# A block-attention and Fourier-mixing kernel: its instruction order replaced as a whole, some e^s - 1 ops and one clear given to GpSimd

## The chip, the cores and the metric

The kernel runs on one core of a Trainium2 chip. The metric is device time in microseconds of one launch. A core has five engines that run side by side and meet through semaphores: TensorE (PE, with weight loads shown apart as PEld), VectorE (DVE), ScalarE (ACT), GpSimd (POOL) and SyncE (SP), which here only issues DMAs. GpSimd issues DMAs too, and each engine takes its instructions in program order.

## The reference, cut to what matters

There are four batches, eight heads, 768 positions and 64 features per head. The first half is attention within blocks of 96 positions, whose keys and values are first mixed across the eight blocks by a Sinkhorn-normalised 8 x 8 matrix P.

```python
for _ in range(5):
    P = exp(P - max(P)); P = P / sum(P, -1); P = P / sum(P, -2)
k_sorted = einsum('bhij,bhjcd->bhicd', P, k_b)
v_sorted = einsum('bhij,bhjcd->bhicd', P, v_b)
attn = softmax(0.125 * q_b @ k_sorted.T)      # inside each block
x = attn @ v_sorted                           # to [4, 768, 512]
```

The second half mixes x by a two-dimensional Fourier transform, normalises each position and adds a feed-forward.

```python
u = x + real(fft(fft(x, axis=1), axis=2))
un = (u - mean(u)) / sqrt(var(u) + 1e-06)
out = u + maximum(un @ w_ch1, 0) @ w_ch2      # 512 -> 2048 -> 512
```

## The kernel before, in words

The work is written as small steps, each a Python generator named `t_` and a letter; each `yield` cuts it into calls. A string ORDER of 1314 tokens says which step is called next; a token such as `x010` makes the next call of step x with the arguments 0, 1, 0. Trailing capital letters choose an engine: A is ScalarE, D is VectorE, P is GpSimd. At the end (the loop over `runs`) every instruction is tied to the one before it on its engine, so ORDER fixes the order of work on TensorE, VectorE, ScalarE, SyncE and GpSimd alike. A second string, SLOTS, gives each tile that is taken from a shared pool its buffer (the eight PSUM banks b0 to b7 among them).

The steps, with the lines that the profile names:

- Sinkhorn (L316 to L324): a chain that alternates between VectorE and ScalarE on a 32 x 64 matrix pw, which SyncE loads first. Two copies of it, pdup (L378, L381), feed J (L389) and D (L448) on TensorE, from which B, T, H and b make the block-diagonal mixing matrices.
- I (L277): two filler matmuls on the identity, which wait for one of Sinkhorn's ten normalisations: `I4` for number 4, and so on. Their result is not used.
- M, Z, s (L425, L432, L463): the mean of v over a block and v minus that mean. The tile vst holds v in two halves of 48 positions, loaded by L229; V loads the second pair of batches.
- v, w (L476, L486, copies at L286 and L288): mixed values into vsf. k (L511) and its copies: mixed keys. q (L306, or L297 and a DMA transpose): transposed queries.
- x (L529, L534): scores on TensorE and their exponential ex on ScalarE, two heads at a time. e (L548): ex - 1, written to the buffer eb in 16 bits; the part that the 1 stands for comes back through an extra row. o (L561, L570, L575): the product with the values, a reciprocal of the sum and the scaled result in r.
- a, A, R, r, f, c, d, p, g: the Fourier parts. f folds r into sums and differences, c and d are the transforms on TensorE (L719, L755, L758), with a reversal of y on VectorE (L739); d leaves u (L769), p copies a part of PSUM (bs, L776) and adds and subtracts it (L782, L784) on the engine of its letter, and g takes the statistics (L791, L795).
- l, n: the norm, four small ops on GpSimd (L799 to L808) and un on ScalarE or VectorE (L816, L819), then a transpose into ut.
- h, y: the feed-forward. h (L843) is four matmuls of 384 columns for one of sixteen slices of the hidden width, evicted through a ReLU by ScalarE (L852) or VectorE (L850); y (L863) is four matmuls of 512 columns, the last of four adds u (L868) and stores. The last tile of all is done as four pieces of 128 columns.
- C loads tables and weights: `C0` the table dtab, its copy on GpSimd (L357), then the four parts of w1 and of w2; `C1` tab, `C2` cs, `C3` lt and rrow. L loads q and k of batches 2 and 3. GpSimd issues the loads of v, q, k, w1 and w2; SyncE the rest.

eb has four buffers, one for each head modulo four. Their zeros around the blocks are set once: three by VectorE (L246), the first instructions that it has, and one by GpSimd (L258). Behind L258, GpSimd sets some constants and issues the loads of q and k of batch 1 (kq, L203).

Digits in a token are batch, head pair (or head, or half) and index: `h00i` is batch 0, half 0, slice 8. Batches overlap: attention of one stands beside the feed-forward of the one before.

Of the kernel before, what the change touches and what calls it, by code (L numbers as in the profile page):

```python
# [18 lines left out]
H = 8  # L19
# [87 lines left out]
def kernel(  # L107
# [18 lines left out]
        "00011101 00010234 50671030 12436570 13541602 05240031 63725241 "  # L126
        "61012052 63475001 25314102 06103012 04513222 10030415 11274602 "
        "53130145 36510210 03210302 01560420 33200075 60111221 22340330 "
        "01276225 10173200 00200653 04210013 13610004 56102525 11621110 "
        "65112701 35471623 05243052 00016450 16110470 21112364 21160323 "  # L130
        "61172420 61372041 64161010 20345245 17630010 04176325 11271652 "
        "37261401 05032102 33560171 00310010 00620057 32036401 11017624 "
        "23213156 23520605 43101204 47051106 01110521 03411070 16502411 "
        "02713260 50732415 00274113 52224760 11003511 22104731 00001210 "
        "17315000 14236220 31041230 03107652 01103651 01547162 30400762 "
        "37631401 07521240 11101501 01641320 27614031 54302100 11023201 "
        "50262732 36000054 07001001 51143120 04353542 00117102 16572110 "
        "40111035 60270456 07453147 352041 "
# [27 lines left out]
    def start(ins):  # L166
        return tc.keep_in_program_order(ins)
# [77 lines left out]
    for n in range(NE - 1):  # L245
        nc.vector.memset(ebuf[n][0:96, :], 0.0)  # L246
# [11 lines left out]
    start(nc.gpsimd.memset(ebuf[NE - 1][0:96, :], 0.0))  # L258
# [281 lines left out]
    def t_e(b, hp, g):  # L540
        for h2 in range(2):
            if h2:
                yield
            e = ebuf[(2 * hp + h2) % NE]
            ed = bass.AP(
                tensor=e.tensor, offset=e[:, S * g:S * g + 1].offset,
                ap=[e[0:96, :].ap[0], [224, 4], [1, BLK]])
            nc.vector.tensor_scalar(ed, exs[b, hp, g, h2], -1.0, None,  # L548
                                    op0=ALU.add)
# [330 lines left out]
    def t_i():  # L880
# [4 lines left out]
        "C0 I4 I5 M00 M01 M02 M03 J M04 M05 C0 B0 C1 B1 B2 D q00A Z0 "  # L885
        "Z0 s02 k00AA H k01AD Z0 s03 q00 k00 k00 k00 x001 k01 b0 s01 "
        "x000 x001 s04 b0 x000 x000 a0 a0 x001 s05 s00 q01D k01 q02D "
        "k01 k02AA q01 e001 k02 k02 v61A v61 v40A e001 v70A v40 v41D "
        "v50D a0 b1 k02 v41 q02 v30A v30 x010 V x010 x010 V T1 v70 "
        "v20A e010 v20 v50 e000 e000 e010 A0 R0 x011 x021 R0 R0 R0 "  # L890
        "q03D q03 R0 R0 x011 x011 x021 v60D v10A v60 v00A k10AA v10 "
        "e011 e011 x021 k03AA R0 v00 x020 x020 k03 k03 k03 o00 o01 "
        "k10 k10 k10 x020 e021 x030 o00 e020 x030 x030 e021 o02 o01 "
        "o00 o01 o03 o02 o03 x031 q11A r1 C2 C3 r0 r1 e030 o03 e020 "
        "o04 k11AA x031 e031 x031 o05 e030 R0 o04 e031 o04 q11 k11 R0 "
        "o02 o05 k11 q10A q13A q13 v51A o07 o07 o05 q10 v51 M10 o06 "
        "v31A k11 x111 x101 x101 x101 v31 M11 o07 o06 f00 o06 f00 "
        "v21A v01A f01 f01 k13AA e101 x110 f02 k13 f02 M12 M13 e101 "
        "f03 f03 M14 v21 x100 x111 x110 x111 e110 c00 L20 f04 x100 "
        "x110 c00 b1 L30 M15 C0 L20 q20 C0 f05 f05 Z1 v01 C0 e111 "  # L900
        "e110 c01 c01 c02 c00 e111 c01 c02 c03 c04 e100 r0 r0 v71A "
        "k12AA c03 q20 c04 d02 v71 v11A x100 d02 p02P d00 p02 d01 k12 "
        "q12A k12 e100 d00 c03 p00P p01P q12 v11 k13 d02 c04 d00 d01 "
        "Z1 c02 d04 p00 k12 k13 d01 p02 p01 p01 p04P Z1 I1 p00 d05 T2 "
        "g02 g01 p05P x121 x121 x131 x131 a1 o13 o10 a1 x121 g00 g01 "
        "x131 C0 g02 g00 l00 l00 l00 l00 e121 o12 I2 x130 e131 o11 "
        "d04 o12 d05 x130 x130 d05 d04 k20AA n001AA o11 q21 I3 e130 "
        "o11 d03 n001 n002AA n001 L21 n000DD o16 n002 p04 o12 n000 "
        "n000 L21 C0 p04 o16 p05 C0 n002 x120 x120 d03 k20 e130 p03P "
        "o13 s15 e120 o13 h00iA h00fD h00f h00i x120 o10 s10 o10 "  # L910
        "h00jD h00j e121 d03 h00cA h00pA h00hA h00h h00p q21 o16 "
        "h00dA e120 k21AA k21 s13 k21 k20 k20 h00c h00kD e131 s12 s14 "
        "x200 k21 h00oA h00nA s11 o14 x200 h00d x200 h00gA o17 h00aA "
        "h00k h00a h00lA wpA h00g p05 C0 o17 o17 o15 h00mA h00bA g05 "
        "o15 o14 o14 wkA h00l h00b wk h00n h00eA h00e o15 f10 h00o wp "
        "y0010 y0020 e200 g04 x201 x201 L30 x211 x211 p03 p03 g03 f11 "
        "f11 g04 f10 f12 h00m C0 g05 g03 l01 f12 e200 f13 y0021 y0022 "
        "l01 l01 x201 weD wbA wb wgD c10 we y0023 l01 q22 f13 n011DA "
        "e201 c10 f14 woA c11 c11 wo y0000 wjD e211 wj x211 y0001 "
        "n011 n011 c12 wg f15 whA wdA y0011 y0002 c13 c12 wh y0023 "  # L920
        "y0023 r1 n012DD f15 n012 y0012 wlA n012 c13 y0013 wcA q22 "
        "wnD waA wa n010DD n010 wl y0003 n010 wd c14 c14 h01aA wn "
        "y0003 wfD q23 q23 T3 y0013 c10 d11 h01oA h01o wiA h01dD h01d "
        "h01lA h01l y0003 y0013 d10 h01pA wc h01a wi h01p wf h01jD "
        "wmD h01gA wm e201 x210 d10 d10 c11 h01g x210 x210 p10P h01j "
        "d12 h01mA k22AD k22 k22 k22 e210 e210 k23DD q31 k23 k23 "
        "h01cA c13 d11 p12P h01c h01hA h01h p11P k23 h01fA h01f e211 "
        "h01iA d12 h01bD d12 p11 h01m h01i h01kA x230 x231 d11 h01b "
        "p12 p12 p11 g11 g12 g11 g12 x220 h01eA x230 h01e x220 x230 "
        "y0110 o22 x231 e231 o20 h01nD h01n o20 h01k o21 p10 p10 o23 "  # L930
        "o23 o20 L31 x220 L31 g10 g10 o23 y0111 y0112 y0120 a1 l10 "
        "l10 l10 l10 o22 o22 y0121 k31AA c14 n101A k31 q31 e230 e220 "
        "A1 c12 x231 o21 o21 k31 x221 n101 R1 e231 R1 n100A n100 "
        "y0100 y0101 q30 R1 R1 R1 n102A n102 x221 y0113 y0113 d13 "
        "y0102 y0122 R1 R1 e230 y0113 x221 e221 k31 d14 R1 R1 r2 r2 "
        "h10iA h10nA h10i d14 q30 k30DD e221 k30 k30 k30 y0123 r2 "
        "e220 y0123 p14P o27 h10eD h10n h10e h10kD o27 d14 y0123 "
        "y0103 d15 o27 h10aA h10a h10dA h10gA h10g h10bA y0103 h10k "
        "p13D p15P h10cA h10c h10hA h10mA h10m h10d q32 d13 d13 y0103 "
        "h10lA h10h h10jD p13 p14 p14 g14 d15 d15 g14 p15 p15 h10fA "  # L940
        "h10f h10oA o26 g15 p13 g13 g13 g15 l11 l11 l11 h10j o26 "
        "h10pD o26 h10b y1010 l11 o24 o24 y1000 h10l o25 n110D o25 "
        "h10o h10p y1011 x311 x311 x311 x301 f21 o25 f21 y1001 n112A "
        "x301 y1020 y1021 o24 f20 f20 n110 r3 e301 n111D y1002 y1012 "
        "f22 f22 f23 f23 c20 c20 y1013 y1022 q32 x300 x301 x300 x310 "
        "y1023 c21 c21 n112 f24 f25 c23 n111 e311 q33 y1013 y1023 c23 "
        "h11cD c22 f25 y1003 y1003 y1023 y1003 c22 c24 x300 h11c c24 "
        "k32DD k33DA k33 k33 e311 x310 k32 k32 d21 k33 p21P k32 d21 "
        "d21 e300 h11fD h11f h11oA e310 d22 d20 p20P h11lA p22P d22 "
        "d22 c24 h11mA c20 r3 h11kA q33 y1013 d20 h11l h11o p22 p22 "  # L950
        "h11m x310 h11hD h11jA h11j g22 o32 x331 e300 x331 h11bA p21 "
        "h11h x331 h11k g22 o32 h11eA h11iA e310 p20 c23 e301 p21 g21 "
        "h11b o32 h11pD h11aD h11a h11e h11i d20 p20 g20 g20 e331 "
        "x330 g21 l20 l20 l20 l20 h11p x321 h11gA h11g h11dA o31 x321 "
        "o30 o31 o31 e321 x321 h11nA h11d n202A y1110 x330 c22 o33 "
        "h11n y1111 y1112 n202 o33 e330 e331 c21 n201A o33 n201 n200D "
        "n200 r3 y1100 y1101 e321 x320 x320 e320 y1113 y1113 o30 "
        "y1120 x320 x330 e330 y1102 y1103 y1121 y1122 y1123 y1103 "
        "h20nA h20aA h20dD h20a d24 p24P y1123 y1123 d24 d24 d23 h20n "
        "h20lD h20l h20pD h20kD p23P h20k o30 h20jA h20j y1103 d25 "  # L960
        "d25 p24 p24 p25P g24 h20fD h20f h20p h20cA h20iD y1113 o34 "
        "h20c h20bA h20b h20eD d23 d23 d25 h20d p23 e320 h20mD o35 "
# [79 lines left out]
```

## Time and profile before

| | before |
|---|---|
| median of 4 runs | 272.01 us (271.62 to 272.39) |
| the profiled execution | 272.08 us, its span 270.3 us |
| busy: PE, DVE, ACT, POOL | 253.4, 197.1, 126.0, 74.7 us |
| share of the span | 94%, 73%, 47%, 28% |
| instructions of PE, DVE, ACT, POOL | 2440, 489, 287, 118 |
| mean granted TensorE clock | 0.987 |
| first h00 matmul | 62.36 us |
| chain that ended last | PE 85%, DVE 9%, ACT 3% |

The costliest groups are the feed-forward's matmuls: L843, 512 of 326 ns in the mean and 89.8 us busy, and L863, 432 of 355 ns and 88.6 us. Matmuls are pipelined, so that a duration is longer than the step from one to the next; four of L843 follow each other in 0.65 us. The e ops, L548, are 64 of 374 ns on VectorE, 22.9 us. The page's rows give line, engine, operation and shapes, then the busy time and the mean of one, then the idle time of the engine ahead of them and what ended it.

### The profile page before, as it was taken

Reading aid. Unit: us, or ns where it says so; the run is one execution under the profiler, and the core shown is the slowest. Engines: PE = TensorE matmul, PEld = TensorE weight load, DVE = VectorE, ACT = ScalarE, POOL = GpSimd, SP = SyncE. Lnnn points to the kernel's source line nnn. Section 1 sums busy time; section 2 is a strip of 40 time slices with the busy share of each in tenths; the row PEclk is TensorE's granted clock in tenths of the full one; section 3 lists DMA queues with packets and bytes.
Section 4 is the critical chain, followed back from the end, with each engine's and each line's share of the span. In section 5 each row is a group of like instructions: output and inputs, shape, how many; then the busy total and the mean of one; then the engine's idle time right before and its main releaser. Section 6 shows DMA issues by size and latency. Waiting matters only on the chain.

```text
span 270.3 us, 6119 instructions
## 1 busy us (share of the span) xinstructions
PE 253.4 (94%) x2440; PEld 157.2 (58%) x2440; DVE 197.1 (73%) x489; ACT 126.0 (47%) x287; POOL 74.7 (28%) x118
## 2 busy tenths in 40 slices
PE   0789889798999999999999999999999999999995
PEld 0279776565656766655655665466466545545554
DVE  6797999989999578868688696458965825912523
ACT  2258898985676476352633565133314312431100
POOL 8912400578721006502220053024200521410000
PEclk9977999999999999999999999999999999999999
DMA  6999999959980231843022610230023023020006
GB/s 120 204 250 205 217 242 242 183 89 174 207 129 14 62 110 29 119 102 83 37 49 45 116 37 10 57 116 4 19 42 116 0 44 133 0 42 19 0 12 223
DMA packets 33138, 26.38 MB, mean 98 GB/s; under 512 B 17395, under 2 KB 28787, under 8 KB 33108
## 3 DMA queue, kind: packets, MB, share of 16 engines
q0 software_dynamic: 11712, 13.63, 30.1%
q1 hardware_dynamic: 21398, 12.36, 17.5%
q8 instruction: 19, 0.31, 0.5%
q14 instruction: 9, 0.07, 0.1%
HBM read 29.00 MB, written 6.29 MB: 131 GB/s over the span
## 4 chain that ended last, share of the span: by engine, by line
PE 85%; DVE 9%; ACT 3%; issue 1%; POOL 1%; DVEq 0%
PE pf L863 31%; PE pf L843 29%; PE pf L719 3%; PE pf L561 3%; PE pf L529 2%; PE pf L425 2%; PE pf L755 2%; PE pf L511 2%; PE pf L758 2%; DVE eb L548 2%; PE pf L277 1%; PE pf L486 1%; PE pf L476 1%; PE pf L306 1%; PE pf L615 1%
## 5 line engine op out<-in xcount | busy, mean ns | idle before, releaser
L843 PE MATMUL pf<-ut,w1sb 128*128 128x384 f16 x512 | 89.8, 326 | 0.2
L863 PE MATMUL pf<-w2sb,hr 128*128 128x512 f16 (+1 forms) x432 | 88.6, 355 | 0.0
L843 PEld LDWEIGHTS <-w1sb 128*128 128x128 f16 x512 | 48.8, 98 | 31.2
L852 ACT ACTIVATE hr<-pf 128x384 f16<-128x384 f32 x78 | 35.7, 493 | 60.3 <-PE pf L843 60.1
L863 PEld LDWEIGHTS <-hr 128*128 128x128 f16 x432 | 38.5, 98 | 37.7
L782 POOL TENSOR_TENSOR u<-u,bs 128x255 f32<-128x255 f32 x21 | 17.6, 845 | 119.9 <-ACT bs L776 69.1
L868 DVE TENSOR_TENSOR u<-pf,u 128x512 f32<-128x512 f32 (+1 forms) x27 | 16.9, 627 | 29.0 <-PE pf L863 28.9
L534 ACT ACTIVATE ex<-pf 96x384 f32<-96x384 f32 x64 | 28.8, 490 | 10.3 <-PE pf L529 8.2
L850 DVE TENSOR_SCALAR hr<-pf 128x384 f16<-128x384 f32 x50 | 26.3, 547 | 7.7 <-PE pf L843 7.6
L548 DVE TENSOR_SCALAR eb<-ex 96x384 f16<-96x384 f32 x64 | 22.9, 374 | 2.6 <-ACT ex L534 2.4
L769 DVE SCALAR_TENSOR_TENSOR u<-r,pf 128x256 f32<-128x256 f16 x48 | 18.2, 411 | 6.3 <-ACT bs L776 3.2
L784 POOL TENSOR_TENSOR u<-u,bs 128x255 f32<-128x255 f32 x21 | 17.7, 848 | 6.5 <-DVE u L769 6.4
L816 ACT ACTIVATE un<-u,nm,ny 128x512 f16<-128x512 f32 x14 | 11.1, 810 | 17.6 <-POOL nm L808 13.4
L791 DVE BATCH_NORM_STATS2 st<-u 128x6 f32<-128x512 f32 x24 | 16.3, 687 | 3.5 <-POOL u L784 3.1
L286 ACT CAST vsf<-pf 96x512 f16<-96x512 f32 x23 | 16.4, 738 | 3.4 <-PE pf L486 3.1
L575 DVE TENSOR_TENSOR r<-pf,rz 128x384 f16<-128x384 f32 x32 | 17.2, 545 | 0.2
L561 PEld LDWEIGHTS <-eb 97*128 97x128 f16 x384 | 14.9, 97 | 3.7 <-DVE eb L548 0.5
L561 PE MATMUL pf<-vsf,eb 97*128 97x65 f16 x384 | 16.4, 194 | 0.3 <-ACT ex L534 0.2
L733 ACT ACTIVATE y<-pf 128x386 f16<-128x386 f32 x16 | 7.4, 498 | 11.3 <-PE pf L719 11.3
L277 PE MATMUL pf<-pack 128*128 128x512 f16 x12 | 4.4, 458 | 8.4 <-DVE pw L324 8.2
L529 PE MATMUL pf<-qt,ksb 64*128 64x96 f16 x256 | 10.0, 208 | 2.0 <-ACT ksb L286 1.4
L776 ACT COPY bs<-pf 128x256 f32<-128x256 f32 x24 | 8.6, 373 | 5.6 <-PE pf L758 3.8
(118 smaller groups left out, 308.5 us busy)
## 6 DMA issues: line engine op xcount, KB each, us to landing
out_dram<-u SPq DMA_DIRECT2D x23, 256.0 KB, 2.3
vst<-in_v_dram POOLq DMA_DIRECT2D x4, 768.0 KB, 11.2
q<-in_q_dram POOLq DMA_DIRECT2D x6, 384.0 KB, 13.1
k<-in_k_dram POOLq DMA_DIRECT2D x6, 384.0 KB, 10.6
w1sb<-in_moe_w_ch_dram POOLq DMA_DIRECT2D x4, 512.0 KB, 17.9
w2sb<-in_moe_w_ch_dram POOLq DMA_DIRECT2D x4, 512.0 KB, 8.2
kq<-in_k_dram POOLq DMA_DIRECT2D x2, 384.0 KB, 14.9
kq<-in_q_dram POOLq DMA_DIRECT2D x2, 384.0 KB, 16.2
```

The lines of the kernel that those rows point to most:

```text
L534: nc.scalar.activation(ex.rearrange("p j (c r) -> p j c r", r=6), pss[h2][0:96].rearrange("p j (r c) -> p j c r", c=16), AF.Exp, scale=SCALE)
L548: nc.vector.tensor_scalar(ed, exs[b, hp, g, h2], -1.0, None, op0=ALU.add)
L561: nc.tensor.matmul(po[:, 65 * T:65 * T + 65], e[:, S * g + 256 * tt + 128 * n: S * g + 256 * tt + 128 * n + 128], vsf[:, vi:vi + D + 1], s ...
L575: nc.vector.tensor_tensor(rt[:, :, D * h:D * h + D], po3[:, :, 0:D], rz[:, :, None].broadcast_to([128, 6, D]), op=ALU.mult)
L769: nc.vector.scalar_tensor_tensor(u[:, o:o + 256].rearrange("p (j n) -> p j n", n=2), rts[b][:, T, o:o + 256].rearrange("p (j n) -> p j n", ...
L782: e.tensor_tensor(u[:, 1:256], u[:, 1:256], bs[:, 1:256], op=ALU.add)
L784: e.tensor_tensor(u[:, 257:512], u[:, 257:512], bs[:, 255:0:-1], op=ALU.subtract)
L843: nc.tensor.matmul(ps, w1sb[:, c, 128 * fc:128 * fc + 128], uns[b, g][:, c, :], start=(c == 0), stop=(c == 3))
L850: nc.vector.tensor_scalar(hr[:, fc, :], ps, 0.0, None, op0=ALU.max)
L852: nc.scalar.activation(hr[:, fc, :], ps, AF.Relu)
L863: nc.tensor.matmul(po, hrs[b, g][:, fc, 128 * tt:128 * tt + 128], w2sb[:, fc, cols], start=(fc == 0), stop=(fc == 15))
L868: nc.vector.tensor_tensor(u[:, cols], po, u[:, cols], op=ALU.add)
```

## The change

Four edits. First, ORDER is written anew as a whole; it has the same number of calls of every step, and the same matmuls. Second, the engine letters in it differ: e now takes two letters, one for each head of the pair, and 34 of its 64 ops are on GpSimd; p goes from 21 on GpSimd and 3 on VectorE to 16 and 8; evictions of h from 78 on ScalarE and 50 on VectorE to 83 and 45; some copies of k, q, v, w and un change sides. Third, SLOTS is new with it. Fourth, VectorE clears two buffers of eb at the start, and GpSimd two.

```diff
-    for n in range(NE - 1):
+    for n in range(NE - 2):
         nc.vector.memset(ebuf[n][0:96, :], 0.0)
...
-    start(nc.gpsimd.memset(ebuf[NE - 1][0:96, :], 0.0))
+    for n in (NE - 2, NE - 1):
+        start(nc.gpsimd.memset(ebuf[n][0:96, :], 0.0))
...
-    def t_e(b, hp, g):
+    def t_e(b, hp, g, e0, e1):
...
-            nc.vector.tensor_scalar(ed, exs[b, hp, g, h2], -1.0, None,
+            eng = nc.vector if (e0, e1)[h2] == "D" else nc.gpsimd
+            eng.tensor_scalar(ed, exs[b, hp, g, h2], -1.0, None,
                                     op0=ALU.add)
...
     ORDER = (
-        "C0 I4 I5 M00 M01 M02 M03 J M04 M05 C0 B0 C1 B1 B2 D q00A Z0 "
-        "Z0 s02 k00AA H k01AD Z0 s03 q00 k00 k00 k00 x001 k01 b0 s01 "
-        "x000 x001 s04 b0 x000 x000 a0 a0 x001 s05 s00 q01D k01 q02D "
-        "k01 k02AA q01 e001 k02 k02 v61A v61 v40A e001 v70A v40 v41D "
...
+        "I1 I3 C1 I2 M00 I4 M01 M02 M03 M04 M05 Z0 J I5 D H B1 B0 Z0 "
+        "C0 s04 b0 s03 Z0 a0 a0 s05 q01A s02 s01 q00A q00 q01 b0 "
+        "k00AA k00 C3 C2 k00 b1 s00 V V k00 k01AD k01 k01 v70D x001 "
+        "B2 x001 v40D x001 k01 x010 x011 x011 x011 a0 v70 v30A v61A "
+        "v61 T1 e001PD L20 v40 x010 A0 e010DD e001 e011DP v30 x010 R0 "
+        "x000 v60A e010 R0 R0 R0 C0 v41D v41 R0 R0 v50D x000 x000 v60 "
+        "q02D k02AA k02 k02 k02 v10A e000PP v10 e000 e011 q02 v00A "
...
```

The fillers I1, I2 and I3, which stood between the calls of d, x and o of batch 0 (at 53 to 59 us of the trace), are the first, second and third of TensorE's work now. In GpSimd's order, two of w1's loads stand behind e101 and the first half of e111 (both of batch 1), the other two behind its second half; no e stood there before. The first call of h00 is the 337th of the string; it was the 355th.

## The prediction

> **What bounds the kernel now.** I read the page's busy tenths first, then the busy time in stretches, then TensorE's waits and the timeline at the places that these name. The columns of the stretches are the bounds in us, the length, and the busy time of PE, PEld, DVE, ACT and POOL (instructions in brackets), then PE's granted clock, the DMA share and GB/s.
>
> ```profile
> PE   0789889798999999999999999999999999999995
> DVE  6797999989999578868688696458965825912523
> PEclk9977999999999999999999999999999999999999
> ```
>
> ```profile
> 16.00:24.00 8.00, 7.21 (x119) 6.42 (x119) 6.55 (x15) 5.78 (x17) 2.60 (x4) 0.57 1.25 244
> 24.00:32.00 8.00, 7.32 (x152) 6.42 (x149) 7.28 (x17) 7.22 (x17) 2.60 (x5) 1.00 1.21 210
> 32.00:40.00 8.00, 7.34 (x188) 6.21 (x184) 7.83 (x28) 7.64 (x17) 0.51 (x1) 1.00 1.14 230
> 40.00:48.00 8.00, 7.25 (x100) 5.17 (x101) 8.00 (x20) 6.94 (x18) 0.00 (x0) 1.00 1.17 248
> 48.00:56.00 8.00, 6.39 (x105) 4.27 (x103) 7.90 (x21) 6.71 (x19) 5.47 (x7) 1.00 0.78 135
> 56.00:64.00 8.00, 7.00 (x102) 4.83 (x102) 7.26 (x23) 7.04 (x18) 6.54 (x11) 1.00 0.96 131
> 64.00:72.00 8.00, 7.62 (x83) 4.78 (x82) 8.00 (x17) 3.92 (x10) 6.31 (x7) 1.00 1.27 204
> 72.00:256.00 184.00, 184.00 (x1485) 108.84 (x1482) 128.11 (x307) 76.08 (x169) 37.73 (x62) 1.00 0.26 59
> ```
>
> From 72 to 256 us PE has no idle time and waits for nobody. No order can gain there; a new one can only lose. What is to be had lies ahead of 72 us. From 24 to 72 us PE is busy 7.32 + 7.34 + 7.25 + 6.39 + 7.00 + 7.62 = 42.9 of 48 us, so 5.1 us idle, while VectorE is busy 46.3 of 48: there it, not PE, sets the pace. PE's waits in that window add up to 4.2 us by name, 3.1 of them for VectorE (the longest 1.3 us for a y reversal, L739) and 1.1 for ScalarE. That is three quarters for VectorE. Ahead of it stands the Sinkhorn chain:
>
> ```profile
> 0.95 2.31 DVE L246 MEMSET eb<- 96x768 uint32 x3 [0.95 <-PEq L1026]
> 3.19 0.15 DVE L316 TENSOR_REDUCE rmax<-pw 32x8 f32<-32x64 f32 x1
> 13.59 0.36 PE L389 MATMUL pf<-pack,pdup 32*128 32x32 f16 x8
> ```
>
> Sinkhorn's first instruction (L316) starts when the third clear ends, though its matrix, issued at 0.73 us, landed 1.6 us later, at 2.3. J (L389) can't start before Sinkhorn ends.
>
> **The change, part by part.** The sum is made against the profiled execution, 272.08 us (span 270.3), which is 0.07 above the median of 272.01.
>
> *A clear moved.* Three clears on VectorE take 2.31 us, one 0.70 with its gap of 0.1; with two, L316 can start at about 2.5 instead of 3.19. The ten normalisations behind it are one chain, so pdup comes 0.7 us sooner: **-0.7 us**. Between 0 (M05 is now ahead of J and may be the later one, below) and 0.8. GpSimd gets another 1.77 us clear (L258) at 9.2 us, and behind it the four kq loads of batch 1 go out at about 12.1 instead of 10.34. Their landing was 15 to 16 us after issue; k10, which reads them, is the 134th call instead of the 101st (30.3 us before), so I charge nothing; without that cover it is 1.8 us.
>
> *The e ops.* Of 64, 34 go to GpSimd. What counts is what stands ahead of the first h00 call, where the feed-forward begins (62.36 us in the trace, 355th call, now 337th). Counting calls of both strings ahead of it, by VectorE's mean rows: e 29 to 12 (17 x 0.374 = -6.4); halves of d -2 (x 0.411 = -0.8); one s, two q reversals of L297, one q copy and one Z fewer (-0.74 - 0.68 - 0.55 - 0.19 = -2.2); two more v copies (+1.5), one p (+1.0), one un (+0.6). VectorE: -6.3 us. ScalarE, the same way: -2.8 (two v copies, four atd, one un fewer; one q, one k copy more). PE's work ahead of h00 is the same within 0.3 us (two k groups more, one a fewer). So the same PE work waits for less VectorE work.
>
> What an e takes on GpSimd, no row shows. Nearest is its one-input copy, 772 ns for 640 elements; with the 240 ns of its three-element tensor_scalar (L799) as the fixed part, 384 elements take 0.56 us. Ends: 0.46 (in proportion to the copy) and 1.28 (in proportion to the two-input add of 255 elements, 848 ns). I take 0.56: 16 of them ahead of h00 are 9.0 us on an engine with time to spare.
>
> But the two engines get in each other's way, and the trace has it:
>
> ```profile
> 62.48 0.74 POOL L784 TENSOR_TENSOR u<-u,bs 128x255 f32<-128x255 f32 x1
> 62.62 0.83 DVE L548 TENSOR_SCALAR eb<-ex 96x384 f16<-96x384 f32 x1
> 63.17 1.53 POOL L782 TENSOR_TENSOR u<-u,bs 128x255 f32<-128x255 f32 x1
> 64.04 0.88 DVE L548 TENSOR_SCALAR eb<-ex 96x384 f16<-96x384 f32 x1
> ```
>
> An e on VectorE has a median of 0.347; begun beside a GpSimd add it took 0.83 and 0.88 and ended 0.2 us after the add. The add beside an s (L463) took 1.53 instead of 0.72. So each collision costs VectorE up to 0.5 us. Instructions of the kinds delayed (e, s, f, y reversals) ahead of h00 and behind the first e: about 33. GpSimd's e ops fill 9.0 of the 36 us from 24 to 60, a quarter: 8 collisions; a wait of 0.35 each (about half of the op and its tail) gives 2.9 us. VectorE's net relief is 6.3 - 2.9 = 3.4 us, and three quarters of it, PE's share of waits for VectorE, reach PE: **-2.5 us**. Ends: 0 and all of PE's idle 5.1.
>
> The Trainium skill speaks against the move: GPSIMD Engine Reference, Engine selection, puts elementwise work on VectorE, GpSimd being about twice as slow with two inputs and near line rate with one. From its 1.03 cycles an element at 1.2 GHz, an estimate for 384 elements is 0.33 us before dispatch, and by that the collisions would be fewer and the gain 0.4 us larger.
>
> *What queues behind them.* An e on GpSimd waits for its ex from ScalarE, and GpSimd takes its work in order: behind e001 stand L20's load and the dtab copy (for d, from 48.5 us; the copy ran at 19.3 before), behind later ones w1's loads and the p adds (for g, and so for un). The e ops' own readers are the o groups. None of it is short by the calls; if it were, PE would wait the 0.56 us of an e, or its 1.28.
>
> *The new order.* I1 to I3 (six fillers of 0.22 us, at 53 to 59 us before) stand at the head now, where PE has nothing else: 0, at best -1.3. GpSimd's loads now stand behind e ops: w1's four loads go out behind e101 and e111 (about 44 to 51 us, before: 30 to 32 and 55.74). The last one, 55.74, was in time for h00 at 62.36, so 0; w2's first load stands 43 calls ahead of y0010, before 87, also 0. If a w1 load is late, PE stands for it. C2 and C3 (0.87 MB) go out near 18 us instead of 35, beside the v and kq loads at 210 to 250 GB/s: up to 4 us on those, hidden as k10 and M10 are later too. M03 to M05 are now ahead of J, behind the second half of v. Evictions of h change from 50 to 45 on VectorE; the end (four 128-column pieces, add, store) is the same: 0.
>
> *The clock.* Eight matmuls of 512 columns took 3.35 us at 10.3 and four 0.97 at 13.9: half speed and full. From 16.7 to 23.5 it was at half again (0.57 in that stretch). Whether the earlier fillers change it I can't tell from one trace: 0, between -3 (half of PE's work there) and +2.7 (below).
>
> The skill's TensorE: Matmul & The Clock Gate, Part 1, has full speed after a window of about 3.4 us of steady work and half after an idle one. By that the M groups would run at full speed from about 10 us, which is hidden behind J's wait.
>
> Sum: 272.08 - 0.7 - 2.5 = **268.9 us**.
>
> **The rivals.** *No net change:* ScalarE, busy 35.6 of 40 us from 24 to 64, is late next, and J is late: v's second half feeds M03 to M05, 2.55 us at half speed. v's first two loads landed 8.6 us after issue in the median and the quickest 7.1, so the second about 10, at 12.0 us; 12.0 + 2.55 = 14.55 against 13.59, +1.0. With a relief of 1.0 left: **272.1**. For it: ScalarE's load; against: it falls by 2.8 too.
>
> *Slower, by the shared port:* GpSimd's e takes the upper end, 1.28 us; 16 fill 20.5 of 36 us, 19 of 33 VectorE instructions collide at 0.5: 9.5 us against 6.3 saved. VectorE is 3.2 us worse, three quarters reach PE: 272.08 - 0.7 + 2.4 = **273.8**. It decides from 13 collisions on. For it: the 0.83 and 0.88 rows; the o groups also wait for the late e. Against: copies on GpSimd are quicker than adds.
>
> *The clock falls* between 48 and 64 us, where PE is least busy and the fillers are gone: 6.8 us at half speed, 80% busy, 2.7 us: **271.6**.
>
> **How the numbers follow.** Forecast (266.3 to 270.9) 0.58; no net change (270.9 to 272.7) 0.17; shared port (to 275) 0.19; clock 0.06. The range goes from 272.08 - 0.7 - 5.1 = 266.3 to the port's 273.8, with some 0.05 below and 0.12 above. Faster by over 0.2% (about what a measurement of this kernel can tell from no change), below 271.47: 0.58 + 0.05 + 0.02 = 0.65; within: 0.09; slower: 0.26.
>
> **What would show it.** L316 at 2.5 us; J at 12.9; 30 e on VectorE and 34 on GpSimd, near 0.56 us; VectorE still 95% busy from 24 to 60 but h00 at 58 to 60; PE's idle time from 24 to 72 near 2.6 us and still none behind. Wrong if GpSimd's e is above 1 us, if VectorE's e is above 0.45 in the mean, if PE shows waits behind 72 us, or if the clock row drops in a second place.

## The result and the profile after

The kernel after takes 273.17 us (median of 33 runs, 271.36 to 275.86). The kernel before, run beside it, takes 272.22 (54 runs, 271.07 to 273.18). The ratio is 1.0037, with an interval of 1.0024 to 1.0051: slower by 1.0 us, where 268.9 was forecast. The profiled execution of after took 272.25 us (span 270.3), 0.9 below its median, so its trace shows only 0.2 us of the loss against the 272.08 of before. What the trace can't show was therefore asked of experiments. A few executions were in a slower state (two of after, two of `old_e1_pool` with its traced one among them, one of before); the ratios leave them out.

Line numbers of after run ahead of those of before by one behind VectorE's clears and by two behind t_e: e is L550, o L563, r L577, d L771, un L821, h L845. The busy tenths of after:

```profile
PE   2979888989999999997999999999999999999995
DVE  6697989999997669777977487759917724702511
PEclk9986999999999999999999999999999999999999
```

Up to 72 us (ten slices and a half) the rows look much as before. A 7 has come up in PE's row in the slice from 121.6 to 128.4 us, where before had a 9. The same stretches as in the prediction:

```profile
16.00:24.00 8.00, 6.65 (x113) 5.61 (x113) 7.32 (x15) 5.82 (x15) 3.20 (x3) 0.63 1.22 258
24.00:32.00 8.00, 7.58 (x163) 6.94 (x162) 6.28 (x15) 6.71 (x16) 5.17 (x6) 0.94 1.24 243
32.00:40.00 8.00, 6.77 (x175) 5.58 (x172) 7.13 (x22) 7.59 (x17) 6.80 (x7) 1.00 1.07 214
40.00:48.00 8.00, 6.66 (x107) 4.85 (x105) 7.64 (x15) 6.70 (x16) 6.85 (x8) 1.00 0.93 147
48.00:56.00 8.00, 7.47 (x123) 4.70 (x118) 7.95 (x22) 6.76 (x18) 6.51 (x7) 1.00 0.94 190
56.00:64.00 8.00, 6.68 (x94) 4.58 (x93) 7.73 (x18) 5.59 (x13) 7.73 (x11) 1.00 0.09 15
64.00:72.00 8.00, 8.00 (x77) 4.84 (x75) 7.46 (x20) 5.18 (x14) 6.29 (x8) 1.00 1.15 180
72.00:256.00 184.00, 182.44 (x1475) 108.66 (x1474) 123.38 (x290) 77.93 (x177) 51.90 (x72) 1.00 0.32 67
```

From 24 to 72 us VectorE does 44.2 us of work instead of 46.3, and GpSimd, the last of the five engine columns, is busy for most of it. PE is busy 43.2 of 48 us instead of 42.9: of 5.1 us idle, 0.2 went. Before's 42.9 hold the six fillers of 53 to 59 us, 1.3 us, which after does ahead of 8 us; so these rows alone don't tell what the relief of VectorE gave TensorE. Behind 72 us, where before had no idle time at all, PE now has 184.00 - 182.44 = 1.56 us of it. The first h00 matmul comes at 61.77 us instead of 62.36, with all parts of the change together, and that lead is gone again by batch 1: the first h11 matmul is at 149.3 instead of 148.1.

The two groups of e, from the groups by line with shapes apart (count, then busy time and mean of one, then the idle time ahead and what ended it):

```profile
L550 POOL TENSOR_SCALAR eb<-ex 96x384 f16<-96x384 f32 x34 | 44.0, 1305 | 38.7 <-ACT ex L535 35.6 <-PE pf L563 1.9 <-DVE pf L649 1.0
L550 DVE TENSOR_SCALAR eb<-ex 96x384 f16<-96x384 f32 x30 | 12.2, 418 | 3.5 <-ACT ex L535 2.8 <-PE pf L563 0.7
```

An e on GpSimd takes 1.31 us in the mean and 1.17 in the median, not 0.56. The 30 on VectorE have a mean of 0.418, where the 64 of before had 0.374. Each of the two new places at which TensorE stands reads off three timelines. First VectorE, then GpSimd, then PE, near 59 us:

```profile
57.64 1.40 DVE L821 TENSOR_SCALAR un<-u,ny,nm 128x512 f16<-128x512 f32 x1 [0.27 <-POOL nm L810]
```

```profile
57.59 2.47 POOL L550 TENSOR_SCALAR eb<-ex 96x384 f16<-96x384 f32 x2
```

```profile
59.10 0.40 PE L832 MATMUL pf<-pack,un 128*128 128x128 f16 x4 [1.29 <-DVE un L821]
```

The un on VectorE takes 0.54 us with GpSimd idle; begun 0.05 us behind two GpSimd e ops it took 1.40, and the transposes of un waited for it. The other place is at 128 us, VectorE first and then PE:

```profile
124.13 1.07 DVE L771 SCALAR_TENSOR_TENSOR u<-r,pf 128x256 f32<-128x256 f16 x3
126.87 0.42 DVE L771 SCALAR_TENSOR_TENSOR u<-r,pf 128x256 f32<-128x256 f16 x1 [1.67 <-DMA out_dram<-u]
...
127.77 0.52 DVE L577 TENSOR_TENSOR r<-pf,rz 128x384 f16<-128x384 f32 x1
```

```profile
128.34 1.46 PE L845 MATMUL pf<-ut,w1sb 128*128 128x384 f16 x8 [1.19 <-DVE r L577]
```

VectorE stands 1.67 us at a d add, because the buffer that the add writes is still being stored to memory. Behind it in VectorE's queue stand the ops of o24 and o25 that free a PSUM bank, and h needs that bank.

The start, VectorE and then PE:

```profile
0.95 1.50 DVE L246 MEMSET eb<- 96x768 uint32 x2 [0.95 <-PEq L1029]
2.38 0.15 DVE L317 TENSOR_REDUCE rmax<-pw 32x8 f32<-32x64 f32 x1
```

```profile
12.03 1.46 PE L426 MATMUL pf<-vst,pack 128*128 128x512 f16 x6 [0.28 <-DMA vst<-in_v_dram]
13.42 0.36 PE L390 MATMUL pf<-pack,pdup 32*128 32x32 f16 x8
```

Sinkhorn starts 0.81 us sooner, as forecast, and pdup comes at 11.61 instead of 12.42. J comes only 0.17 us sooner: M03 to M05 stand ahead of it and wait for v's second half at 12.0 us.

### The profile page after: what moved, and what is told of

Same layout as the page of the kernel before. It is cut to its first block, busy times and chain, and to the rows that moved or that the text cites. A ratio compares the mean times of both kernels' runs of the same rounds, so it can differ in the third digit from the quotient of the medians.

```text
span 270.3 us, 6118 instructions
## 1 busy us (share of the span) xinstructions
PE 253.9 (94%) x2440; PEld 156.9 (58%) x2440; DVE 189.1 (70%) x457; ACT 128.3 (47%) x294; POOL 108.6 (40%) x143
## 4 chain that ended last, share of the span: by engine, by line
PE 76%; DVE 12%; DMA 5%; POOL 2%; issue 2%; ACT 2%; DVEq 0%; POOLq 0%
PE pf L865 30%; PE pf L845 28%; DMA vst<-in_v_dram 4%; PE pf L563 3%; PE pf L721 3%; PE pf L530 2%; PE pf L487 1%; PE pf L757 1%; PE pf L760 1%; DVE u L771 1%; DVE st L793 1%; DVE eb L550 1%; DMA out_dram<-u 1%; PE pf L617 1%; PE pf L610 1%
## 5 line engine op out<-in xcount | busy, mean ns | idle before, releaser
L845 PE MATMUL pf<-ut,w1sb 128*128 128x384 f16 x512 | 89.5, 326 | 1.5 <-DVE r L577 1.2
L845 PEld LDWEIGHTS <-w1sb 128*128 128x128 f16 x512 | 49.0, 98 | 34.0 <-issue 2.2
L854 ACT ACTIVATE hr<-pf 128x384 f16<-128x384 f32 x83 | 38.5, 494 | 61.9 <-PE pf L845 61.7
L550 POOL TENSOR_SCALAR eb<-ex 96x384 f16<-96x384 f32 x34 | 44.0, 1305 | 38.7 <-ACT ex L535 35.6
L852 DVE TENSOR_SCALAR hr<-pf 128x384 f16<-128x384 f32 x45 | 23.6, 545 | 14.6 <-PE pf L845 14.6
L784 POOL TENSOR_TENSOR u<-u,bs 128x255 f32<-128x255 f32 x16 | 12.2, 767 | 47.9 <-DVE u L771 28.5
L771 DVE SCALAR_TENSOR_TENSOR u<-r,pf 128x256 f32<-128x256 f16 x48 | 18.4, 412 | 8.2 <-DMA out_dram<-u 4.1
L563 PE MATMUL pf<-vsf,eb 97*128 97x65 f16 x384 | 16.6, 194 | 1.2 <-issue 0.8
L563 PEld LDWEIGHTS <-eb 97*128 97x128 f16 x384 | 14.8, 97 | 4.8 <-issue 1.2
L577 DVE TENSOR_TENSOR r<-pf,rz 128x384 f16<-128x384 f32 x32 | 17.2, 545 | 0.4
L287 ACT CAST vsf<-pf 96x512 f16<-96x512 f32 x22 | 15.8, 737 | 1.4 <-PE pf L477 0.9
L550 DVE TENSOR_SCALAR eb<-ex 96x384 f16<-96x384 f32 x30 | 12.2, 418 | 3.5 <-ACT ex L535 2.8
L818 ACT ACTIVATE un<-u,nm,ny 128x512 f16<-128x512 f32 x11 | 8.7, 809 | 12.3 <-DMA ut<-un 7.2
L287 ACT CAST ksb<-pf 128x384 f16<-128x384 f32 x27 | 12.6, 494 | 3.1 <-PE pf L512 3.1
L786 POOL TENSOR_TENSOR u<-u,bs 128x255 f32<-128x255 f32 x16 | 12.5, 786 | 1.9 <-DVE u L771 1.9
L821 DVE TENSOR_SCALAR un<-u,ny,nm 128x512 f16<-128x512 f32 x13 | 8.2, 639 | 6.7 <-DMA ut<-un 4.4
## 6 DMA issues: line engine op xcount, KB each, us to landing
k<-in_k_dram POOLq DMA_DIRECT2D x6, 384.0 KB, 10.3
```

The costliest lines, as they stand in the source:

```text
L287: nc.scalar.copy(dst, src)
L550: eng.tensor_scalar(ed, exs[b, hp, g, h2], -1.0, None, op0=ALU.add)
L563: nc.tensor.matmul(po[:, 65 * T:65 * T + 65], e[:, S * g + 256 * tt + 128 * n: S * g + 256 * tt + 128 * n + 128], vsf[:, vi:vi + D + 1], s ...
L577: nc.vector.tensor_tensor(rt[:, :, D * h:D * h + D], po3[:, :, 0:D], rz[:, :, None].broadcast_to([128, 6, D]), op=ALU.mult)
L771: nc.vector.scalar_tensor_tensor(u[:, o:o + 256].rearrange("p (j n) -> p j n", n=2), rts[b][:, T, o:o + 256].rearrange("p (j n) -> p j n", ...
L845: nc.tensor.matmul(ps, w1sb[:, c, 128 * fc:128 * fc + 128], uns[b, g][:, c, :], start=(c == 0), stop=(c == 3))
```

## The experiments

Sixteen kernels ran, in four groups, each with five rounds beside the kernel before. All ratios are to the kernel before, where after stands at 1.0037. The short diffs are against before for the names with old, and against after for those with new.

**Which part holds the loss.** Four kernels do or undo one part each. `new_e_dve`:

```diff
-        "v61 T1 e001PD L20 v40 x010 A0 e010DD e001 e011DP v30 x010 R0 "
+        "v61 T1 e001DD L20 v40 x010 A0 e010DD e001 e011DD v30 x010 R0 "
...
```

> The changed kernel with all 64 e ops on VectorE (order, buffers and clear as changed). Price theory (an e on GpSimd takes 1.16 to 1.3 us instead of 0.56, and the port waits hand VectorE's relief back): 270.5 to 272.2, at least 1 us below the changed kernel, whose PE waits of 1.45 us at 59 us (un of batch 0 on VectorE beside two GpSimd e ops) and 1.35 us at 128 us go. Order theory (the new order and buffers bring the waits, whatever engine e runs on): 273 or more, since VectorE, busy 93% from 24 to 64 us, gets 34 more ops of 0.35 us. VectorE's e back at 0.35 to 0.37 in the mean under the price theory.

Measured 274.96 us, 1.0097 [1.0067, 1.0128]. With all e ops on VectorE the new order is slower still, by 0.6%. The new order without its GpSimd e ops loses 1% against before, and the e ops give part of it back.

`old_e_pool` is the reverse, before's order with after's engines for e:

```diff
+            eng = nc.vector if (e0, e1)[h2] == "D" else nc.gpsimd
...
-        "k01 k02AA q01 e001 k02 k02 v61A v61 v40A e001 v70A v40 v41D "
+        "k01 k02AA q01 e001PD k02 k02 v61A v61 v40A e001 v70A v40 v41D "
...
```

> The kernel before with the changed kernel's letters for e, so 34 of 64 on GpSimd, in the old order and buffers. Price theory: slower than before by 1 to 4 us, the GpSimd e at 1.2 to 1.4 us and PE waiting for o's inputs between 28 and 72 us. Order theory: faster than before by 0.5 to 2 us, because VectorE loses 34 ops of 0.35 us. The old order was not laid out for it, so a loss here alone would not settle it.

Measured 284.17 us, 1.0428 [1.0399, 1.0456]. In the old order the same 34 ops on GpSimd cost 4%. TensorE stands 4.5 us, until 50.9 us, for f5; why, the next group shows.

`new_clear_back` and `old_clear` take the clear by itself:

```diff
-    for n in range(NE - 2):
+    for n in range(NE - 1):
         nc.vector.memset(ebuf[n][0:96, :], 0.0)
...
-    for n in (NE - 2, NE - 1):
-        start(nc.gpsimd.memset(ebuf[n][0:96, :], 0.0))
+    start(nc.gpsimd.memset(ebuf[NE - 1][0:96, :], 0.0))
```

> The changed kernel with the clear back on VectorE (three there, one on GpSimd). If the sooner Sinkhorn is worth its 0.8 us: slower than the changed kernel by 0.5 to 0.8. If J waits for the M groups now (v's second half lands at 12.0 us and M05 ends at 13.4, J began at 13.42 with pdup ready at about 12.4): slower by 0.0 to 0.3, with J at 13.5 to 13.8.

> The kernel before with the clear alone moved to GpSimd. If the head hangs on Sinkhorn: faster than before by 0.5 to 0.8 us, J at 12.8. If the head hangs on M, v and TensorE's half clock as well: by 0.0 to 0.4.

`new_clear_back` (the diff above) measured 272.9 us, 1.0015 [0.9991, 1.0038]; `old_clear` (the diff reversed, in before) 272.82 us, 1.0023 [1.0001, 1.0045]. Moving the clear gains nothing in either order. In `old_clear` the trace says where the 0.8 us goes. PE's timeline in it, then the same group in before and in `old_no_fill` (below), which has the clears of before:

```profile
13.20 0.39 PE L390 MATMUL pf<-pack,pdup 32*128 32x32 f16 x8
...
22.28 0.53 PE L512 MATMUL pf<-bdk,k 128*64 128x128 f16 x12 [1.73 <-DMA k<-in_k_dram]
```

```profile
22.43 0.85 PE L511 MATMUL pf<-bdk,k 128*64 128x128 f16 x12
```

```profile
22.20 0.53 PE L511 MATMUL pf<-bdk,k 128*64 128x128 f16 x12 [1.03 <-DMA k<-in_k_dram]
```

Sinkhorn is 0.8 us sooner (J, 0.4), and then the k group of heads 4 to 7 waits for its load, which lands at 22.24 us. In before the same load landed at 22.11 and the group started at 22.43, so that the load hid just behind the work. But before's trace has TensorE at half speed there, from 16.7 to 23.5 us. `old_no_fill` ran there at full speed, and its group already waits 1.03 us for this load without any clear moved; the 1.73 us of `old_clear` are about that and the 0.7 of a clear. The next bound stood there all the time, with 0.3 us of room at half speed and none at full.

**What an e on GpSimd costs, and what stands behind it.** `new_e_half` lets GpSimd do two of the four blocks of each of its e ops and leaves the other half out:

```diff
+            nb = 4 if (e0, e1)[h2] == "D" else 2
...
-                ap=[e[0:96, :].ap[0], [224, 4], [1, BLK]])
+                ap=[e[0:96, :].ap[0], [224, nb], [1, BLK]])
...
-            eng.tensor_scalar(ed, exs[b, hp, g, h2], -1.0, None,
+            eng.tensor_scalar(ed, exs[b, hp, g, h2][:, 0:nb], -1.0, None,
```

> The changed kernel, but each of the 34 e ops on GpSimd does two of its four blocks; the other half is left out. An op should then take near the 0.56 us that the prediction took. If the price of a GpSimd e was the failing step: 268.5 to 270.5 us, and the waits behind 100 us gone. If the new order has its waits whatever an e costs: 272.0 to 273.0, still with the waits of about 1 us at 39.7, 46.6 and 59.1 us.

Measured 271.39 us, 0.9983 [0.9965, 1.0002]: 1.5 us faster than after, and between the two expectations. Part of it goes with fewer half-speed stretches of the clock (below; 1.2 on average instead of 1.9). In its trace TensorE's waits for un at 59 us and for r at 128 us are still there, 1.1 and 1.4 us, so that the gain doesn't come from these two. One such half takes 0.69 us in the median, 192 elements against 1.17 for 384. By these two points the op costs 0.21 us plus 2.5 ns an element; they differ in the number of blocks too, so that a price by the block isn't told apart. The price matters, but at about half of it the time is still 2.5 us above the forecast.

`old_e1_pool` gives GpSimd four e ops only, in the old order, and `old_e1_behind` the same four, but with the first one behind the loads that stood behind it:

```diff
-        "f03 f03 M14 v21 x100 x111 x110 x111 e110 c00 L20 f04 x100 "
-        "x110 c00 b1 L30 M15 C0 L20 q20 C0 f05 f05 Z1 v01 C0 e111 "
+        "f03 f03 M14 v21 x100 x111 x110 x111 e110PP c00 L20 f04 x100 "
+        "x110 c00 b1 L30 M15 C0 L20 q20 C0 f05 f05 Z1 v01 C0 e111PP "
...                          # e by its letters, as in old_e_pool; DD at every other e
```

```diff
-        "f03 f03 M14 v21 x100 x111 x110 x111 e110PP c00 L20 f04 x100 "
-        "x110 c00 b1 L30 M15 C0 L20 q20 C0 f05 f05 Z1 v01 C0 e111PP "
+        "f03 f03 M14 v21 x100 x111 x110 x111 c00 L20 f04 x100 "
+        "x110 c00 b1 L30 M15 C0 L20 q20 C0 e110PP f05 f05 Z1 v01 C0 e111PP "
```

> The kernel before with four e ops alone on GpSimd: e110 and e111 of batch 1, between 44 and 49 us, where GpSimd has nothing to do until 50.4 us and PE later waits 1.3 us for VectorE's y reversal at 52.9. Relief theory: 270.8 to 272.0, PE's wait for L739 below 0.8 us. Port theory (f's two-input ops stand beside, VectorE gains nothing, GpSimd's p ops start late): 272.5 to 274, f4 and f5 above 1.1 and 0.7 us.

> The kernel before with the same four e ops on GpSimd as in the run that lost 2.5% (e110 and e111), but the first call of e110 stands behind the loads of q, k and w1 instead of ahead of them. Queue theory: the loss came from the loads' issue standing behind an e that waits for its ex in GpSimd's in-order queue; the loads go out again at 22 to 31 us, the 5.8 us wait of c (L720) for f5 is gone, and the time is 271.9 to 273.0 us. Port theory: it came from four GpSimd e ops of 1.2 us that hold up VectorE; the time stays above 277 us.

`old_e1_pool` measured 279.56 us, 1.0248 [1.0216, 1.028]; `old_e1_behind` 272.81 us, 1.0036 [1.0018, 1.0055]. Four ops of 1.2 us can't take 6.8 us by what they last. GpSimd's timeline in `old_e1_pool`, then VectorE's and PE's:

```profile
44.12 1.20 POOL L549 TENSOR_SCALAR eb<-ex 96x384 f16<-96x384 f32 x1 [21.60 <-ACT ex L534]
45.28 1.60 POOL L188 DMA_DIRECT2D q<-in_q_dram  x2
```

```profile
50.18 0.50 DVE L297 COPY qr<-q 128x768 f16<-128x768 f16 x1 [4.73 <-DMA q<-in_q_dram]
```

```profile
51.50 1.80 PE L720 MATMUL pf<-cs,pmt 128*128 128x193 f16 x10 [5.65 <-DVE pmt L708]
```

GpSimd takes its queue in order, and its first e waits for its ex from 22.5 to 44.1 us. Behind it the loads of q wait to be issued: in before they went out at 22.25 and 29.40. A copy of q on VectorE then waits 4.7 us for the data, f5 stands behind that copy, and TensorE behind f5. One early wait was handed through three queues. With the e behind the loads GpSimd's timeline reads:

```profile
22.11 0.76 POOL L188 DMA_DIRECT2D q<-in_q_dram  x1
28.55 0.75 POOL L188 DMA_DIRECT2D q<-in_q_dram  x1 [5.68 <-PE pf L306]
...
43.88 1.20 POOL L549 TENSOR_SCALAR eb<-ex 96x384 f16<-96x384 f32 x1 [12.75 <-ACT ex L534]
```

The same e still waits, until 43.88, but nothing that is needed soon stands behind it, and 2.1 of the 2.5% are gone. What is left, 0.4%, comes with the four e ops on GpSimd in an order that wasn't made for them; it wasn't taken apart. `old_e_pool` shows the same two waits (VectorE 3.9 us for q, TensorE 4.5 us for f5), so that this queue has a part in its loss of some 11.6 us too; the rest of that stays open.

**The waits of the new order.** `new_e_late_dve` puts the e ops of batches 2 and 3 back on VectorE; `new_un_free` only the two of 57.6 us that stand beside un; `new_d15_late` puts three ops of o24 and o25 ahead of the d add that waits for the store, with SLOTS moved along so that the tiles keep their buffers.

```diff
-        ... f13 n010 e210PD y0003 c10 ... x201 x200 e201PP h01nD h01n ...
+        ... f13 n010 e210DD y0003 c10 ... x201 x200 e201DD h01nD h01n ...
...
```

> The changed kernel with the e ops of batches 2 and 3 back on VectorE (14 of the 34 on GpSimd), those of batches 0 and 1 as changed. If the loss behind 72 us (1.6 us of PE idle, the longest wait 1.2 us at 128 us for r, behind a late e) comes from GpSimd's e: 271.5 to 272.4. If it comes from the order: 273 to 274.5, with waits of 0.5 to 1.5 us at 122, 174 and 189 us as with all e on VectorE.

```diff
-        ... x121 n002AA e131PD Z1 n001DA d05 o12 d03 o11 n001 p03P e121PD ...
+        ... x121 n002AA e131DD Z1 n001DA d05 o12 d03 o11 n001 p03P e121DD ...
```

> The kernel after with the first halves of e131 and e121 (the two GpSimd e ops at 57.6 us) on VectorE. Port theory of the wait of 1.45 us at 59.1 us: un on VectorE takes 0.6 us instead of 1.40, TensorE's wait for it falls below 0.6 us, and the time falls by 0.6 to 1.0 us to 272.1 to 272.6. Rival, that the order has the next wait ready (ScalarE, whose ex and copies stand behind un): the wait at 59.1 shrinks and comes back within 15 us; 273.0 to 273.4 us.

```diff
-        ... d13 d14 o25 d15 o24 p15 o25 o24 x231 ...
+        ... d13 d14 o25 o24 o25 o24 d15 p15 x231 ...
```

> The kernel after with three VectorE ops of o24 and o25 (two reciprocals and one scaled result) ahead of the first add of d15, which at 125.2 us waits 1.67 us for the store of an earlier output out of its buffer u. Queue theory: r comes 1.3 us sooner, TensorE's wait of 1.35 us at 128 us falls below 0.4, and the time falls by 0.7 to 1.2 us, to 271.9 to 272.5. Rival: the wait comes back behind it (the late d15, p15 and g15 hold up the norm of batch 1), or the price of GpSimd's late e ops stands behind it: 272.9 to 273.4.

`new_e_late_dve` measured 273.75 us, 1.006 [1.0036, 1.0084], no better than after. The wait for r at 128 us is gone from its trace, but TensorE is idle 2.25 us behind 72 us instead of 1.56, 1.33 of it at 121.7 us for ScalarE's ex: with the late e ops on VectorE other waits come. `new_un_free` measured 271.63 us, 0.9996 [0.9972, 1.002], 0.4% faster than after and more than I expected. VectorE, GpSimd and PE in it:

```profile
57.10 0.94 DVE L821 TENSOR_SCALAR un<-u,ny,nm 128x512 f16<-128x512 f32 x1
```

```profile
57.04 0.71 POOL L784 TENSOR_TENSOR u<-u,bs 128x255 f32<-128x255 f32 x1
```

```profile
58.10 0.40 PE L832 MATMUL pf<-pack,un 128*128 128x128 f16 x4 [0.93 <-DVE un L821]
```

The next GpSimd op, a p add, has moved up beside un and holds it for 0.4 us instead of 0.86. un still takes 0.94 us, not the 0.6 that I expected, and TensorE's wait for it falls from 1.29 to 0.93 us, 0.36 less. This alone isn't 1.1 us; the two e ops are also done more than 1 us sooner for whoever reads them (the second at 58.7 us instead of 60.1), and this kernel's runs had fewer half-speed stretches of the clock (below). How the rest divides between these two wasn't measured.

`new_d15_late` measured 272.31 us, 0.9999 [0.9979, 1.0018], 0.4% faster than after, as the queue theory had it. VectorE and PE:

```profile
125.50 0.52 DVE L577 TENSOR_TENSOR r<-pf,rz 128x384 f16<-128x384 f32 x1
126.89 0.42 DVE L771 SCALAR_TENSOR_TENSOR u<-r,pf 128x256 f32<-128x256 f16 x1 [0.87 <-DMA out_dram<-u]
```

```profile
125.73 3.59 PE L845 MATMUL pf<-ut,w1sb 128*128 128x384 f16 x21
```

The add still waits until 126.89 for the store, but r is done 2.3 us sooner, and PE's h matmuls run through. TensorE's idle time behind 72 us falls from 1.56 to 0.99 us. The store was never the trouble, only what stood behind it.

`new_J_first` and `new_J_only` put J ahead of M03 to M05:

```diff
-        "I1 I3 C1 I2 M00 I4 M01 M02 M03 M04 M05 Z0 J I5 D H B1 B0 Z0 "
+        "I1 I3 C1 I2 M00 I4 M01 M02 J D M03 M04 M05 Z0 I5 H B1 B0 Z0 "   # new_J_first
+        "I1 I3 C1 I2 M00 I4 M01 M02 J H B1 B0 M03 M04 M05 Z0 I5 D Z0 "   # new_J_only
```

> The kernel after with J and D ahead of M03 to M05, which wait for the second half of v at 12.0 us. If J's lateness is what kept the 0.8 us that Sinkhorn gained, J starts near 12.1 us, the first k group (17.96 us) and h00 come 0.5 to 1.0 us sooner, and the time is 272.1 to 272.7. Rival, that loads (k at 15.9 and 22.1 us) and VectorE's work ahead of h00 set the pace: J comes sooner and h00 does not; 272.9 to 273.4 us.

> The kernel after with J and its readers H, B1 and B0 ahead of M03 to M05; D and the filler I5 keep their places and banks. If J's lateness holds back what Sinkhorn gained, J starts near 12.1 us, VectorE does B1 and B0 in its idle 1.4 us there, h00 comes 0.4 to 0.8 us sooner: 272.3 to 272.8. Rival: what follows is set by D (14.5 us), the loads (k at 15.9 and 22.1 us) and VectorE's work behind them: J comes sooner, h00 stays within 0.3 us, 272.9 to 273.4.

`new_J_first` measured 280.55 us, 1.0288 [1.0242, 1.0333], and answers another question than the one it was made for. SLOTS hands out buffers in the order of the calls; with D ahead of I5 the two exchanged PSUM banks, and the filler then had to wait until D's readers on VectorE had done with the bank. PE's timeline:

```profile
24.51 1.03 PE L278 MATMUL pf<-pack 128*128 128x512 f16 x2 [5.09 <-DVE bdv L453]
```

`new_J_only` keeps the banks, by a SLOTS moved along. It measured 272.51 us, 1.0034 [1.0012, 1.0057], like after. PE in it:

```profile
12.14 0.36 PE L390 MATMUL pf<-pack,pdup 32*128 32x32 f16 x8 [1.13 <-DVE pdup L379]
...
14.48 1.94 PE L449 MATMUL pf<-pack,pdup 32*128 32x32 f32 x16
...
17.97 0.84 PE L512 MATMUL pf<-bdk,k 128*64 128x128 f16 x24
```

J comes 1.3 us sooner than in after (13.42), D at 14.48 (14.47) and the first k group at 17.97 (17.96). In both kernels D stands behind J, the filler I5 and M03 to M05, which wait for v at 12.0 us; only their order differs. So J's lateness was not what held back the 0.8 us, as far as these rows go. The time is less clear: the median lies only 0.3 us above that of before beside it, in the range expected if J did matter, and the first h00 comes at 61.1 us instead of 61.8, in an execution at full clock, where after's ran at half speed from 18.1 to 24.9 us. A gain of a few tenths of a microsecond isn't excluded.

**The fillers and the clock.** `old_no_fill` leaves the six matmuls of I1 to I3 out (nothing reads them); `old_fill_early` issues them at the head of TensorE's work, as the new order does; `new_no_fill` leaves them out of the new order.

```diff
-        idle_mm(2, ph[n])
+        idle_mm(0 if n in (1, 2, 3) else 2, ph[n])
```

```diff
+    for n in (1, 2, 3):        # old_fill_early, ahead of the loop over ORDER, besides the diff above
+        early = psum.tile([128, 512], F32, tag="b7", bufs=1, name=f"early{n}")
+        ...                    # the two matmuls of idle_mm(2, ph[n]) into early
```

> The kernel before without the matmuls of I1, I2 and I3 (six fillers at 53 to 59 us; their result is not used). If they hold the clock: more stretches at half speed than before in some executions, near 60 us, and 0.3 to 1.0 us slower. If the clock doesn't hang on them: the same within 0.3 us or up to 0.6 faster, PE having 1.3 us less to do there.

> The kernel before with the six filler matmuls of I1 to I3 issued at the head of TensorE's work (in a PSUM bank of their own) instead of at 53 to 59 us. If they merely cost their time where they stood, 271.0 to 271.5 us, as without them. If the earlier start of steady matmuls moves the half-speed stretch, it shows in the granted clock ahead of 30 us and in a time outside 270.7 to 271.8; if they weren't a cost, 272.0 to 272.3.

> The kernel after without the six filler matmuls of I1 to I3 at its head (their result is not used). If they cost nothing where TensorE has no other work: 273.0 to 273.4, and as many half-speed stretches as in the kernel after. If an early start of steady matmuls brings more half-speed stretches (2.6 in the mean against 1.2 when they were moved to the head of the old order), without them the mean number falls from 1.9 to near 1.2 and the time by about 0.5 us, to 272.4 to 272.9.

Measured: `old_no_fill` 271.17 us, 0.9975 [0.9955, 0.9996]; `old_fill_early` 272.29, 0.9998 [0.9977, 1.0019]; `new_no_fill` 273.41, 1.0049 [1.0024, 1.0074]. Where they stood they cost 0.7 us (0.1 to 1.2 by the interval). At the head of the old order the time is that of before again; its interval overlaps that of `old_no_fill`, and executions with as many half-speed stretches take about the same in both (one: 271.36 and 271.02 us; three: 272.38 and 272.45). At the head of the new order they cost nothing that shows, and leaving them out there did not bring fewer half-speed stretches, as I had thought it might.

What they have to do with the clock stays open. The trace of after has it at half speed from 18.1 to 24.9 us (the column 0.50):

```profile
18.10:21.50 3.40, 2.52 (x48) 2.01 (x43) 3.40 (x9) 3.17 (x8) 1.01 (x2) 0.50 1.28 221
21.50:24.90 3.40, 3.40 (x46) 3.08 (x44) 2.41 (x4) 2.85 (x7) 3.09 (x3) 0.50 1.21 289
```

Taking the clock as full or half, as in these rows, a run's mean granted clock gives its time at half speed, span x 2 x (1 - clock). That time gathers in steps of about 3.4 us (clocks of 0.994, 0.987, 0.981 and 0.975 give 3.2, 7.0, 10.3 and 13.6 us), which I count as stretches. Over 110 runs beside the experiments, before has none in 33 (271.52 us in the mean), one in 19 (271.73) and two in 58 (272.57), 1.2 on average. After has never none in 32: one in 11 runs (272.50), two in 15 (273.15), three in 4 (274.08) and four in 2 (274.47), 1.9 on average. With equal numbers after is 0.6 to 0.8 us slower; the other 0.3 us or so, an estimate from these means, goes with the more frequent stretches. `old_no_fill` has 1.2, `old_fill_early` 2.6 and `new_no_fill` 2.2, so that the place of the fillers alone doesn't set it, and I have no run that tells what does.

**Do the repairs add up?** `new_three` joins `new_un_free`, `new_d15_late` and `new_no_fill`, by their diffs above.

> The kernel after with three repairs at once: the two e ops beside un on VectorE, o24 and o25 ahead of the first add of d15, and no fillers at the head. If the order is at fault in these places only, the parts add up: 271.6 (un alone) less 0.7 to 1.2 less 0 to 0.5, 270.0 to 270.9, faster than both kernels. If each repair only uncovers the next wait: 271.3 to 272.

Measured 270.93 us, 0.997 [0.995, 0.999]: faster than before by 0.3% and than after by 0.7%. Against after the three alone were -0.41%, -0.38% and +0.12%; their sum is -0.67%, and so is what was measured (0.997 / 1.0037 = 0.9933). The single terms are each uncertain by some 0.2 to 0.3%, so that the close agreement is partly luck. The trace shows less independence than the sum: the waits at 59 and 128 us shrink or go, and the first h00 comes at 60.3 us instead of 61.8, but TensorE is still idle 1.75 us behind 72 us, 1.0 of it at 184.5 us behind a ReLU eviction on VectorE. So single places of the new order cost time, and one repaired wait let another come up. Like `old_no_fill` (271.17) this version beats both kernels; it is still 2 us above the forecast.

## Why the prediction was wrong

The direction was wrong. Step by step:

- **What bounds the kernel.** Right that TensorE waits for nobody behind 72 us, and right that "a new one can only lose" there. But the sum then charged the new order **nothing** for it. This is the first step that failed: behind 72 us it lost 1.56 us in the trace, and the wait at 128 us alone was worth 1.0 us (`new_d15_late`). A wait of VectorE that was harmless in the old order (2.3 us for an output store, its longest there) stands ahead of a PSUM bank in the new one.
- **A clear moved, -0.7.** Sinkhorn came 0.81 us sooner, and none of it arrived (`new_clear_back`, `old_clear`). In the old order the k load at 22.2 us was next, with 0.3 us of room at half speed and none at full. In the new one it wasn't J alone, which I had named (`new_J_only`): D stands at 14.5 us with J early or late, behind the M steps that wait for v. That this holds the time was not tested. I had the landing of the k load in the trace and didn't put it against the start of its reader.
- **The e ops, -2.5.** The largest term and the second step that failed. GpSimd's e took 1.17 us and not 0.56. The fixed part that I took, 0.24, was right (0.21 measured); the 0.83 ns an element that I took from a 16-bit copy was not, 2.5 were measured, by two points, for 32 bits in and 16 out. The upper end, 1.28, was the nearer one. The relief of VectorE was 2.1 us from 24 to 72 instead of 3.4. TensorE's idle time there fell to 4.8 us, not to the 2.6 that I named, and h00 came 0.6 us sooner with all parts together, no more than the fillers cost where they had stood (0.7, `old_no_fill`). `new_e_half` prices the term: halving these ops gives 1.5 us, clock included. Still their move is a gain within the new order: without it that order is 0.6% slower.
- **Collisions, 8 at 0.35.** Of VectorE's 30 e ops 12 ran beside a GpSimd op and took 0.17 us longer in the mean, less than I charged. But a sum was the wrong tool: two GpSimd e ops met the one un that TensorE was about to need, and that one cost 0.86. The mean of VectorE's e rose only from 0.374 to 0.418, inside my sign of 0.45. A mean doesn't show a collision on the path.
- **What queues behind them.** "If it were, PE would wait the 0.56 us of an e, or its 1.28." Wrong in kind: what is handed on is the e's own wait for ex, 21.6 us in `old_e1_pool`, and the price was 2.1% in the old order. The new order has its loads placed so that this doesn't happen, which I had read rightly.
- **Fillers and clock, 0 each.** Moving the fillers to the head was worth nothing, as said. For the clock, about 0.3 us of the loss is more frequent half speed, within the bounds given but with a cause that I don't know.

The rival "slower, by the shared port" ended near, at 273.8, and its condition, e at 1.28, nearly came true; yet its mechanism, many small delays of VectorE, isn't what happened. VectorE had less work and less delay than that, and the two places whose repair gave time back are single ones. Of the signs, GpSimd's e above 1 us and waits of PE behind 72 us spoke, and both named the failed steps.

Two of its sums don't come out. With an e of 0.33 us instead of 0.56 its own way of counting gives 5 collisions and a gain larger by 0.9 us, not 0.4. And its four cases take up the whole of the chances, so that nothing is left for the 0.05 below 266.3 that it adds to "faster".

## What to carry to other kernels

Moving an op to another engine moves its wait too: ask first what stands behind it in that engine's queue, DMA issues above all, and not only how long the op takes. When an order is written anew, the stretch in which the busiest engine waits for nobody is where it can lose, and a wait that was harmless turns costly by what is placed behind it. Before a chain is shortened, put the landing time of the next load beside the start of its reader: the difference is all that can be gained.

## What the hardware showed unexpectedly

Beside a GpSimd op, only some of VectorE's ops grow. In the trace of after (mean with GpSimd idle and with a GpSimd op beside it): un 0.54 and 0.80 us, e 0.35 and 0.52, a y reversal 0.25 and 0.44, and, less clearly, f on 1152 elements (L682) 0.75 (one op alone) and 0.81, at most 1.08. But r (0.55, 0.54), the d adds (0.42, 0.41), the ReLU eviction (0.55, 0.55) and the statistics (0.69, 0.69) do not. The growing ones read and write SBUF alone; of the others r, d and the eviction read PSUM, and the statistics read SBUF and still didn't grow. The Trainium skill (SBUF — State Buffer, section "SBUF: two separate sides") has the rule that fits: the port pair of VectorE and GpSimd is locked for a whole instruction, against VectorE ops in a two-port performance mode or with two SBUF inputs, the latter only where the GpSimd op reads SBUF. By it the ops to be kept away from a GpSimd op are the fast SBUF ones, and the evictions may stand beside it. That the statistics run outside such a mode is what the rule would need; no run here shows it.

The same skill (GPSIMD Engine Reference, Engine selection) calls one-input work on GpSimd roughly line rate. The measured 1.17 us for 384 elements, by the two points above 2.5 ns for each and 0.21 us fixed, speaks against it for this op: the estimate from that page was 0.33 us.
